# Spectral tiles as rows of one tile, with butterflies, mirror sums and filter products on two tiles an operation

## The chip, the cores and the metric

The kernel runs on one core of one Trainium2 chip. The metric is the device time of one execution in microseconds. The kernel before takes 454.19 us, the median of 3 runs (453.86 to 454.76). One further execution was taken with the hardware profiler; its own time was 452.46 us, and the span of its instructions 450.7 us. Line numbers such as L568 are lines of the kernel before, except in rows of the changed kernel's order, where they are lines of the changed kernel.

## The reference, cut to what matters

```python
xn = _layernorm(x, axis=-1)                     # x: [1, 2048, 448]
# branch A: a spectral filter
X = jnp.fft.rfft2(xn, axes=(-2, -1))
X = X * (w_r + 1j * w_i)                        # weights [2048, 225]
yA = jnp.fft.irfft2(X, s=(2048, 448), axes=(-2, -1))
# branch B: a gated network, F = 1792
gate = xn @ W_gate;  up = xn @ W_up
h = jnp.where(gate > 0, gate, 0) * up
yB = h @ W_down
return x + yA + yB
```

## The kernel before, in words

**Branch B is the long work of TensorE (PE).** Every fp32 product is made from fp16 parts (high times high, high times low, low times high). The 1792 hidden columns are cut into 14 blocks in groups of 5, 5 and 4, and the 2048 tokens into four chunks of 512. One *gate-and-up unit* is a block and a chunk: 20 to 24 matmuls of 512 columns into the two banks of a `gu` buffer, of which there are two. After it ScalarE (ACT) takes the relu (`g`, L1028), VectorE (DVE) multiplies by the up bank (`g`, L1032), ACT writes the high half of the result (`h`, L1036) and DVE the low half (`h`, L1040). The `gu` buffer is free again when the DVE's multiplication (L1032) has read it. The down products (`dn`, 448 columns) of a chunk follow when its group's units are through.

**Branch A is the background work.** Forward, each of 16 token residues has a transform along the columns and one along the sequence, on PE (`fx` banks); between them and behind them DVE does the rest in fp32: sums over eight rows (`eight_a`, `eight_b`, with the quarter turns in `turn`), and four levels of butterflies over the 16 residues (`f_y1`, `stage2`, `stage3`, `stage4`, all but the first through `bfly` and `rotate`). A spectral tile holds 464 fp32 numbers a partition: 8 column groups, 2 components (real, imaginary), 29 columns. There are 18 such buffers (`ybuf`), each a tile of its own, handed out from the list `free`. A DVE operation that treats the components apart works on 232 numbers, one on a whole tile on 464. Then each pair of frequencies k and k + 8 has its mirror sums (`pair`, through `add_sides`, with the other half fetched by DMA in `swap`), the product with the filter (`wmul`), and the way back: `inv1`, `stage2`, `stage3`. Row 32 of the partitions goes to a small side calculation (`row`), fetched by `row_in`.

**The last stage has eight steps p = 0 to 7.** Each takes the DVE chain of `i_join` (last butterfly, into a `wst` buffer), `i_pair`, `i_mix` in two halves (`eight_a`, `eight_b`), `i_lo` (`vt`, L815), then a sequence transform on PE (`i_sdft`, 48 matmuls of 64 columns, `fx<-im,vt`), ACT and DVE unfolding its result (`i_part`, L834; `i_unfold`, `yu`, L839), the halves of that (`i_pqhi` on ACT, L844; `i_pqlo` on DVE, `wf`, L849), and a column transform on PE (`i_ddft`, 48 matmuls of 56 columns, `fx<-idc_t,wf`). There is one pair of `fx` banks.

**What sets the order.** Opening and main loop give PE its units. The background stands in a list of items, each with a cost in microseconds (`bf` for butterflies, 1.09 to 1.74). At each unit a planner lets through as many items as its credit pays for. What is then recorded is reordered engine by engine by the framework's scheduler, and the result is a fixed queue for each engine: DVE cannot take a background item ahead of an L1032 that stands before it. All loads and stores are issued from SP's queue, in order.

## Time and profile before

| | |
|---|---|
| median of 3 runs | 454.19 us (453.86 to 454.76) |
| profiled execution, its own time | 452.46 us |
| its span | 450.7 us, mean granted TensorE clock 0.985 |
| PE busy | 427.8 us (95%), 3254 matmuls |
| DVE busy | 394.4 us (88%), 952 instructions |
| ACT busy | 252.8 us (56%), 508 instructions |
| POOL busy | 32.2 us (7%) |

The table is part 1 of the profile's page. Shares are averages over an opening (the first 15 us), a long middle in which PE and DVE are both busy, the eight steps of the last stage (from about 314 us), and an end in which PE works alone. The PE row says only that a matmul was under way; where PE is at its full rate a 512-column matmul starts every 0.216 us and a 448-column one every 0.189 us.

### The profile page before, as it was taken

To read this page: it belongs to the slowest core of one execution; us is meant where nothing else is said; L and a number is where in the kernel's file an instruction comes from. 1 tells how busy PE (TensorE), PEld (TensorE's weight loads), DVE (VectorE), ACT (ScalarE), POOL (GpSimd) and SP (SyncE) were. 2 spreads that over 40 slices of the span, in tenths; PEclk is the share of its full clock that TensorE was granted. 3 is DMA by queue.
4 is the path that set the end of the run, shared out by engine and by line. 5 is a ranking of instruction groups with operands and counts; after the bars stand their busy time and mean duration, and the time that the engine had idled before them with its cause. 6 is when DMAs were issued, how large, how long until landed. Compare 5 with 4: busy or idle time off the path is not lost.

```text
span 450.7 us, 8697 instructions
## 1 busy us (share of the span) xinstructions
PE 427.8 (95%) x3254; PEld 203.4 (45%) x3254; DVE 394.4 (88%) x952; ACT 252.8 (56%) x508; POOL 32.2 (7%) x72
## 2 busy tenths in 40 slices
PE   6999999999999999999999999979999973999997
PEld 2644544444444444444444444434545432444544
DVE  6898898997987998999999999999998989958513
ACT  6897392387359746615434553935675663563630
POOL 1140030031001401000000010010000000000000
PEclk9999999999999999999999999999999995999999
DMA  8769948015002235334330310022122112300212
GB/s 263 243 165 291 373 118 123 2 36 72 3 2 93 67 117 155 81 89 123 87 84 1 100 27 1 1 55 53 29 50 70 37 35 51 105 22 1 83 42 81
DMA packets 37722, 38.63 MB, mean 86 GB/s; under 512 B 18928, under 2 KB 33072, under 8 KB 37680
## 3 DMA queue, kind: packets, MB, share of 16 engines
q1 hardware_dynamic: 37680, 38.09, 30.8%
q8 instruction: 25, 0.41, 0.4%
q14 instruction: 17, 0.14, 0.1%
HBM read 23.20 MB, written 3.67 MB: 60 GB/s over the span
## 4 chain that ended last, share of the span: by engine, by line
PE 51%; DVE 38%; ACT 6%; issue 2%; DMA 2%; SPq 0%; DVEq 0%; ACTq 0%
PE gu L476 31%; PE dn L476 13%; PE fx L476 4%; DVE h L1040 3%; DVE g L1032 3%; DVE y L568 2%; DVE y L569 2%; DVE wt L928 2%; ACT junk L219 2%; DVE y L665 2%; DVE y L668 2%; DVE y L583 2%; DVE y L706 1%; DVE y L584 1%; DVE y L707 1%
## 5 line engine op out<-in xcount | busy, mean ns | idle before, releaser
L476 PE MATMUL gu<-T,wt 128*128 128x512 f16 (+2 forms) x1250 | 270.9, 377 | 4.5 <-DVE g L1032 4.5
L476 PEld LDWEIGHTS <-wt 128*128 128x128 f16 (+1 forms) x1250 | 111.4, 98 | 148.3 <-issue 29.1
L476 PE MATMUL dn<-wdt,h 128*128 128x448 f16 x624 | 127.5, 353 | 0.0
L476 PEld LDWEIGHTS <-h 128*128 128x128 f16 x624 | 60.2, 98 | 57.9 <-issue 0.8
L1036 ACT ACTIVATE h<-g 128x512 f16<-128x512 f32 x56 | 35.1, 627 | 76.7 <-DVE g L1032 76.6
L1032 DVE SCALAR_TENSOR_TENSOR g<-gu,g 128x512 f32<-128x512 f32 x56 | 38.2, 683 | 14.3 <-ACT g L1028 14.2
L1040 DVE TENSOR_TENSOR h<-g,h 128x512 f16<-128x512 f32 x56 | 38.3, 685 | 10.0 <-ACT h L1036 9.9
L1028 ACT ACTIVATE g<-gu 128x512 f32<-128x512 f32 x56 | 32.8, 585 | 17.7 <-PE gu L476 17.7
L1068 ACT ACTIVATE xy<-dn,dsc 128x448 f32<-128x448 f32 x44 | 27.3, 624 | 12.8 <-PE dn L476 12.8
L1057 ACT ACTIVATE dn<-xy,dinv 128x448 f32<-128x448 f32 x44 | 27.5, 631 | 0.5
L928 DVE SCALAR_TENSOR_TENSOR wt<-wst,wsc,wt 128x512 f16<-128x512 f32 x28 | 20.3, 742 | 2.6 <-ACT wt L924 2.6
L222 POOL PARTITION_ALL_REDUCE wm<-wm x15 | 9.0, 598 | 161.0 <-ACT junk L219 161.0
L924 ACT ACTIVATE wt<-wst,wsc 128x512 f16<-128x512 f32 x28 | 19.1, 713 | 1.8 <-DVE wsc L229 1.8
L219 ACT ACTIVATE junk<-wst 128x512 bf16<-128x512 f32 x28 | 17.4, 620 | 1.3 <-DMA wst<-in_wgu 1.1
L810 ACT ACTIVATE vt<-wst,fsc 128x928 f16<-128x928 f32 x8 | 8.8, 1099 | 10.8 <-DVE wst L467 10.8
L957 ACT ACTIVATE wdt<-wdst,wds 128x448 f16<-128x448 f32 x14 | 8.7, 658 | 8.5 <-DVE wds L953 8.5
L569 DVE TENSOR_TENSOR y<-y,y 128x464 f32<-128x464 f32 x21 | 13.3, 633 | 0.1
L568 DVE TENSOR_TENSOR y<-y,y 128x464 f32<-128x464 f32 x21 | 13.3, 632 | 0.1
L657 ACT ACTIVATE wf<-wf 128x116 f32<-128x116 f32 x16 | 4.5, 293 | 15.8 <-DMA wf<-in_wf 15.8
L839 DVE SCALAR_TENSOR_TENSOR yu<-fx,yu 128x512 f32<-128x512 f32 x16 | 11.0, 687 | 2.6 <-ACT yu L834 2.3
L860 ACT ACTIVATE fx<-xy,fsc 128x448 f32<-128x448 f32 x14 | 8.8, 629 | 7.9 <-DVE yu L839 7.9
L291 DVE BATCH_NORM_STATS2 bst<-y 128x6 f32<-128x448 f32 x16 | 9.2, 617 | 4.3 <-DMA y<-in_xr 4.3
(164 smaller groups left out, 506.2 us busy)
## 6 DMA issues: line engine op xcount, KB each, us to landing
wst<-in_wgu SPq DMA_DIRECT2D x28, 256.0 KB, 4.7
wf<-in_wf SPq DMA_DIRECT2D x16, 232.0 KB, 2.8
sw<-y SPq DMA_DIRECT2D x64, 58.0 KB, 2.0
sw<-wst SPq DMA_DIRECT2D x32, 116.0 KB, 2.2
y<-in_xr SPq DMA_DIRECT2D x16, 224.0 KB, 4.9
xy<-in_x SPq DMA_DIRECT2D x16, 224.0 KB, 5.0
out<-xy SPq DMA_DIRECT2D x15, 224.0 KB, 1.9
wdst<-in_wd SPq DMA_DIRECT2D x14, 224.0 KB, 4.6
```

The lines of the kernel that those rows point to most:

```text
L219: A.activation(mt([128, 512], BF16, "junk")[:, 0:src.shape[-1]], src, AF.Square, scale=SQ, accum_out=acc)
L476: r = P.matmul(*a, **k)
L568: V.tensor_tensor(t, a, b, op=OP.add)
L569: V.tensor_tensor(d, a, b, op=OP.subtract)
L924: A.activation(w[:, 0:4, :], wst[f, g], AF.Copy, scale=wsc[f, g])
L928: V.scalar_tensor_tensor(w[:, 4:8, :], st, sc, w[:, 0:4, :], op0=OP.mult, op1=OP.subtract)
L1028: last["A"] = A.activation(g1s[f, q], hps[f, q][:, 0, :], AF.Relu, scale=2.0 ** -22).ins
L1032: last["V"] = V.scalar_tensor_tensor(g1, hps[f, q][:, 1, :], 2.0 ** -22, g1, op0=OP.mult, op1=OP.mult).ins
L1036: A.activation(ht[f, q][:, 0, :], g1s[f, q], AF.Copy)
L1040: V.tensor_tensor(h[:, 1, :], g1s.pop((f, q)), h[:, 0, :], op=OP.subtract)
L1057: A.activation(dps[n2][:, 0:D], xy[n2], AF.Copy, scale=dinv[:, g:g + 1])
L1068: last["A"] = A.activation(xy[n2], dps[n2][:, 0:D], AF.Copy, scale=dsc[:, g:g + 1]).ins
```

## The change

The 18 spectral buffers become rows of one tile `yb`, and within a tile the components come first (2 components, 8 groups, 29 columns), so that one component is 232 numbers in a row. `joint` gives two buffers as one operand: any two rows of `yb`, in either order, are a regular stride. With that, `stage2`, `stage3`, `inv1`, `pair` and `wmul` take two tiles (928 numbers, or twice 232) in one DVE operation. A butterfly needs fewer buffers: its difference is written over one of its inputs. The tiles `eo` (two buffers) and `bw` become one tile `eb`, so that two of the three turns of the forward `eight_b` are done together. The joined butterflies come at other places of the list: `join2` for residues 0 and 2 at once (earlier 0 alone, then 2), for 1 and 3 at once, `join3` only then for the one half with all of its pairs; on the way back likewise. The planner's costs stay what they were for the same work (twice `bf` for a joined item). The low half `i_pqlo` is one operation of 1024 numbers. In `ln_lo` of two chunks a second DVE operation of 64 columns is replaced by a copy on ACT. `i_join`, whose output keeps the old layout, now needs four operations of 232 where it had two of 464, in six of its eight steps.

```diff
-    ybuf = [mt([128, NG, 2, KC], F32, f"y{i}") for i in range(18)]
+    yb = mt([128, 18, 2, NG, KC], F32, "y")
+    ybuf = [yb[:, i] for i in range(18)]
+    yi = {id(t): i for i, t in enumerate(ybuf)}
+    def joint(ts):
+        if len(ts) == 1:
+            return ts[0]
+        i, j = yi[id(ts[0])], yi[id(ts[1])]
+        return yb[:, i:j + 1:j - i] if j > i else (yb[:, i:j - 1:j - i] if j else yb[:, i::j - i])
...
-        for d, a, b in o:
-            if n2 % 4 in CHUNKS[2:]:
-                V.scalar_tensor_tensor(d, a, rst[n2 % 4, n2 // 4, "r"][0], b, op0=OP.mult, op1=OP.subtract)
-            else:
+        if n2 % 4 in CHUNKS[2:]:
+            d, a, b = o[0]
+            V.scalar_tensor_tensor(d, a, rst[n2 % 4, n2 // 4, "r"][0], b, op0=OP.mult, op1=OP.subtract)
+            A.activation(w[:, 8], w[:, 16], AF.Copy)
+        else:
+            for d, a, b in o:
                 V.tensor_tensor(d, a, b, op=OP.subtract)
...
+            u, v = (both[:, i:j + 1:j - i] for i, j in ((fi + 5, wi + 3), (fi + 6, wi + 7)))
+            turn(lambda c: rows[:, :, x[c]], u, v[:, :, ::-1], sgn)
...
-    def bfly(a, b, p, sgn):
+    def bflies(sa, sb, p, sgn):
+        st = [free.pop(0) for _ in sa]
+        a, b, t = joint(sa), joint(sb), joint(st)
         if p == 0:
-            t, d = free.pop(0), free.pop(0)
             V.tensor_tensor(t, a, b, op=OP.add)
-            V.tensor_tensor(d, a, b, op=OP.subtract)
-            free.extend((a, b))
-            return t, d
+            V.tensor_tensor(b, a, b, op=OP.subtract)
+            free.extend(sa)
+            return st, sb
...
+    def level(far, k, p, ks, sgn, src, dst, *js):
+        sa, sb = ([cur.pop((src, j + d, k)) for j in js] for d in (0, far))
+        for x, o in zip(ks, bflies(sa, sb, p, sgn)):
+            for j, t in zip(js, o):
+                cur[dst, j, x] = t
...
+        V.tensor_tensor(t, x, bc[0], op=OP.mult)
+        V.tensor_tensor(x, x, bc[1], op=OP.mult)
+        V.tensor_tensor(comp(t, 0), comp(t, 0), comp(x, 1), op=OP.subtract)
+        V.tensor_tensor(comp(t, 1), comp(t, 1), comp(x, 0), op=OP.add)
...
-    def pair(key, sgn):
-        add_sides(cur[key], sw.pop(key), sgn)
+    def pair(sgn, *keys):
+        add_sides(joint([cur[k] for k in keys]), sw.pop(keys[0]), sgn, comp)
...
-            V.scalar_tensor_tensor(o, t, f, a, op0=OP.mult, op1=OP.add)
-            V.scalar_tensor_tensor(d, t, -f, a, op0=OP.mult, op1=OP.add)
+            for c in range(2):
+                for x, g in ((o, f), (d, -f)):
+                    V.scalar_tensor_tensor(comp(x, c), comp(t, c), g, comp(a, c), op0=OP.mult, op1=OP.add)
...
-        y = yu.pop(p)
-        for b in range(2):
-            V.tensor_tensor(pgh[p + 8 * b][:, 1], y[:, b], pgh[p + 8 * b][:, 0], op=OP.subtract)
+        t = state["pg"]
+        V.tensor_tensor(t[:, 1], yu.pop(p), t[:, 0], op=OP.subtract)
...
-    extra = {1: [(ln_chunk, 1)], 2: [(join2, 0), (rows_in, 3)], 3: [(ln_chunk, 3)], 4: [(join2, 2), (join3, 2)],
-             6: [(join2, 1)]}
+    extra = {1: [(ln_chunk, 1)], 2: [(rows_in, 3)], 3: [(ln_chunk, 3)], 4: [(join2, 0, 2)]}
...
-    join2(3)
-    join3(3)
+    join2(1, 3)
+    join3()
```

The change also moves instructions, since the scheduler starts from other items. The built order of the two kernels differs at two places that matter for what follows. Both lie in the last stage, at the steps p = 3 and 4.

On DVE, before, from the unfolding of step 3 (`yu`) to the low half `i_pqlo` of step 3 (`wf`) and the L1032 of the next unit (`g_4918`):

```order
L1032 SCALAR_TENSOR_TENSOR g_4761<-gu,g_4761 128x512
L839 SCALAR_TENSOR_TENSOR yu<-fx,yu 128x512
L1040 TENSOR_TENSOR h<-g_4761,h 128x512
L839 SCALAR_TENSOR_TENSOR yu<-fx,yu 128x512
L444 TENSOR_TENSOR wst<-wst 128x2x232
L446 TENSOR_TENSOR wst<-wst 128x2x2x116
L448 TENSOR_TENSOR wst<-wst 128x3x116
L449 TENSOR_TENSOR wst<-wst 128x3x116
L849 TENSOR_TENSOR wf<-yu,wf 128x512 x2
L461 TENSOR_TENSOR wst<-wst 128x116
```

and in the changed kernel, the same stretch (L1064 is the multiplication that was L1032, L871 the unfolding, L881 the low half):

```order
L1064 SCALAR_TENSOR_TENSOR g_4611<-gu,g_4611 128x512
L1072 TENSOR_TENSOR h<-g_4611,h 128x512
L871 SCALAR_TENSOR_TENSOR yu<-fx,yu 128x512 x2
L463 TENSOR_TENSOR wst<-wst 128x2x232
L1064 SCALAR_TENSOR_TENSOR g_4768<-gu,g_4768 128x512
L465 TENSOR_TENSOR wst<-wst 128x2x2x116
L467 TENSOR_TENSOR wst<-wst 128x3x116
L468 TENSOR_TENSOR wst<-wst 128x3x116
L881 TENSOR_TENSOR wf<-yu,wf 128x1024
L477 TENSOR_TENSOR wst<-wst 128x116
```

The multiplication of the next unit (`g_4768`) now stands ahead of the low half of step 3; before, it (`g_4918`) stood six rows behind it, past the end of the piece shown.

On ACT, before, the same stretch (L834 is `i_part`, L844 `i_pqhi`, L1028 the relu of a unit, L876 what moves the column transform's result out):

```order
L834 ACTIVATE yu<-fx 128x512
L1036 ACTIVATE h<-g_4761 128x512
L860 ACTIVATE fx<-xy,fsc 128x448
L844 ACTIVATE wf<-yu 128x1024
L860 ACTIVATE fx<-xy,fsc 128x448
L1028 ACTIVATE g_4918<-gu 128x512
L876 ACTIVATE xy<-fx,fsc 128x2x224 x2
L1036 ACTIVATE h<-g_4918 128x512
L810 ACTIVATE vt<-wst,fsc 128x32x29
```

and in the changed kernel (L866 is `i_part`, L877 `i_pqhi`, L1060 the relu):

```order
L866 ACTIVATE yu<-fx 128x512
L1060 ACTIVATE g_4768<-gu 128x512
L892 ACTIVATE fx<-xy,fsc 128x448
L877 ACTIVATE wf<-yu 128x1024
L892 ACTIVATE fx<-xy,fsc 128x448
L1068 ACTIVATE h<-g_4768 128x512
L908 ACTIVATE xy<-fx,fsc 128x2x224 x2
L842 ACTIVATE vt<-wst,fsc 128x32x29
```

The relu of that unit has moved from behind the high half of step 3 to directly behind `i_part`. On PE's queue the same shift reads as counts: between the sequence transform of step 3 and its column transform there were 24 `gu` matmuls and are now 4; the other 20 stand earlier. From there on PE's queue holds the same in both kernels: column transform 3, sequence transform 4, column transform 4 with nothing between them, then 20 `gu` and 4 `dn` matmuls, then sequence transform 5.

More of the change, by code (lines that the diff above doesn't have):

```diff
@@ L588, in f_y1 @@
+        free.extend(st)
+        return sb, sa
     def f_y1(n2):
@@ L767, in i_join @@
         a, b = cur.pop(("i3", 0, p)), cur.pop(("i3", 1, p))
[L768 removed]
+        o, d = (u[:, :, :, KC * i:KC * (i + 1)].rearrange("p g c k -> p c g k") for i in range(2))
         if p == 0:
```

220 lines of the change are left out of this document (111 added, 109 removed).

## The prediction

> **What bounds the kernel now.** I read the shares of the page first, then PE's waits, then the stretches around those waits, then single rows. In the page's list of engines the columns are busy time, share and instructions; its slices follow.
>
> ```profile
> PE 427.8 (95%) x3254; PEld 203.4 (45%) x3254; DVE 394.4 (88%) x952; ACT 252.8 (56%) x508; POOL 32.2 (7%) x72
> ...
>
> ```
>
> PE is never far from busy, DVE nearly so. What matters is therefore when PE stands still, and for whom. PE's waits (us in total, times, longest):
>
> ```profile
> PE gu L476 <- DVE g L1032: 4.5, 3, 2.8
> PE fx L476 <- ACT fx L860: 4.4, 1, 4.4
> PE fx L476 <- ACT vt L810: 3.7, 1, 3.7
> PE fx L476 <- DVE vt L815: 1.6, 1, 1.6
> ```
>
> Two kinds. In the long middle DVE is late three times with freeing a `gu` buffer, 4.5 us. And in the last stage PE waits about 10 us for the chain of steps 3 to 5. Stretches (length, busy time of PE, PEld, DVE, ACT, POOL, granted clock, DMA):
>
> ```profile
> 270.00:285.00 15.00, 15.00 (x77) 6.97 (x76) 14.87 (x42) 7.53 (x16) 0.71 (x1) 1.00 0.01 2
> 285.00:300.00 15.00, 12.16 (x60) 5.42 (x59) 14.90 (x34) 10.18 (x23) 1.54 (x2) 1.00 0.15 33
> 360.00:375.00 15.00, 9.33 (x154) 4.92 (x154) 13.66 (x31) 7.91 (x12) 0.00 (x0) 0.84 0.14 34
> 375.00:390.00 15.00, 10.45 (x159) 5.92 (x154) 13.82 (x32) 6.71 (x10) 0.00 (x0) 0.71 0.39 100
> 390.00:405.00 15.00, 15.00 (x165) 7.48 (x164) 10.19 (x24) 10.15 (x16) 0.00 (x0) 1.00 0.09 32
> ```
>
> Between 270 and 300 us DVE has next to no idle time: it limits by its sum of work. Between 360 and 390 us it idles 2.5 us and PE 10.2, and the clock falls: there a chain that goes from PE to ACT and DVE and back limits. From 390 us PE is alone at full rate. PE, in time, through that place (start, us, operation, [idle before]):
>
> ```profile
> 361.63 0.87 PE L476 MATMUL fx<-im,vt 64*128 64x64 f16 x48
> 362.44 5.03 PE L476 MATMUL gu<-T,wt 128*128 128x512 f16 x24
> ...
> 372.52 0.29 PE L476 MATMUL fx<-im,vt 64*128 64x64 f16 x4 [3.68 <-ACT vt L810]
> 374.45 1.36 PE L476 MATMUL fx<-im,vt 64*128 64x64 f16 x44 [1.65 <-DVE vt L815]
> 380.18 0.28 PE L476 MATMUL fx<-idc_t,wf 64*128 64x56 f16 x4 [4.37 <-ACT fx L860]
> 380.64 1.25 PE L476 MATMUL fx<-idc_t,wf 64*128 64x56 f16 x44 [0.18 <-DVE wf L849]
> 381.82 5.44 PE L476 MATMUL gu<-T,wt 128*128 128x512 f16 x20
> 387.10 0.92 PE L476 MATMUL dn<-wdt,h 128*128 128x448 f16 x4
> 387.95 0.87 PE L476 MATMUL fx<-im,vt 64*128 64x64 f16 x48
> ```
>
> The sequence transform of step 3 ends at 362.50, that of step 4 at 375.81, that of step 5 starts at 387.95. Between the first two stand 24 `gu` matmuls, between the others 20 and 4 `dn`; the rest of the time PE waits.
>
> **What the change saves on DVE.** DVE starts, one after the other (start, duration):
>
> ```profile
> 251.30 0.40 DVE L671 TENSOR_TENSOR y<-y,y 128x232 f32<-128x232 f32 x1
> 251.61 0.39 DVE L670 TENSOR_TENSOR y<-y,y 128x232 f32<-128x232 f32 x1
> ...
> 252.24 0.45 DVE L706 SCALAR_TENSOR_TENSOR y<-sw,mask,y 128x232 f32<-128x232 f32 x1
> 252.61 0.45 DVE L707 SCALAR_TENSOR_TENSOR y<-sw,mask,y 128x232 f32<-128x232 f32 x1
> 252.98 0.63 DVE L568 TENSOR_TENSOR y<-y,y 128x464 f32<-128x464 f32 x1
> 253.53 0.63 DVE L569 TENSOR_TENSOR y<-y,y 128x464 f32<-128x464 f32 x1
> ```
>
> From start to start 232 numbers take 0.31 us, 464 take 0.55, and 232 with the mask 0.37. So 232 numbers more cost 0.24, and 0.07 is paid per operation: two operations of 464 (1.10) become one of 928 (estimate 0.55 + 2 x 0.24 = 1.03). With the mask, two of 232 (0.74) become one of 464, which the last stage has:
>
> ```profile
> 358.69 0.69 DVE L706 SCALAR_TENSOR_TENSOR wst<-sw,mask,wst 128x464 f32<-128x464 f32 x1
> 359.30 0.69 DVE L707 SCALAR_TENSOR_TENSOR wst<-sw,mask,wst 128x464 f32<-128x464 f32 x1
> ```
>
> 0.61, so 0.13 less. Counted in the built order: 116 plain operations disappear into others (20 of L568/L569, 24 of L575 to L578, 16 in rotations, 32 in the filter product, 16 turns, 8 of L849), 116 x 0.07 = 8.1; 16 with the mask, 2.1; eight of 64 columns go to ACT, 8 x 0.2 = 1.6 (duration 0.292 less the 0.08 by which neighbours overlap in the rows above); `i_join` gains 12, -0.8. Then dependence: an operation that reads what the one just before it wrote starts later.
>
> ```profile
> L815 DVE SCALAR_TENSOR_TENSOR vt<-wst,fsc,vt 128x464 f16<-128x464 f32 x16 | 10.5, 698 | 2.3 <-ACT vt L810 2.3
> ...
> L388 DVE SCALAR_TENSOR_TENSOR tt<-y,rs,tt 128x64 f16<-128x64 f32 x8 | 2.3, 292 | 0.0
> ```
>
> ```profile
> 364.98 0.63 DVE L444 TENSOR_TENSOR wst<-wst 128x464 f32<-128x464 f32 x1
> 365.53 0.63 DVE L446 TENSOR_TENSOR wst<-wst 128x464 f32<-128x464 f32 x1
> 366.20 0.52 DVE L448 TENSOR_TENSOR wst<-wst 128x348 f32<-128x348 f32 x1
> ```
>
> L446 needs nothing of L444 and comes after 0.55; L448 needs L446 and comes after 0.67. Joined pairs stand next to what they depend on more often (the order has 77 such neighbours before, 92 after): 15 x 0.12 = 1.8 lost. **DVE has about 8.1 + 2.1 + 1.6 - 0.8 - 1.8 = 9.2 us less work.** That is no gain by itself; PE's idle time is what it can buy.
>
> The Trainium skill (VectorE: DVE Perf Modes, section The DRAIN you can't avoid) says that the next operation cannot start until the pipe is empty; by that a merged pair of 232 would save 2 x 0.39 - 0.63 = 0.15, and DVE some 17 us in place of 8.1. The rows disagree: L569 starts 0.08 before L568 has ended.
>
> **The middle.** The three stalls:
>
> ```profile
> 154.80 2.53 PE L476 MATMUL gu<-T,wt 128*128 128x512 f16 x11 [1.09 <-DVE g L1032]
> ...
> 258.63 1.67 PE L476 MATMUL gu<-T,wt 128*128 128x512 f16 x7 [0.57 <-DVE g L1032]
> ...
> 296.22 3.95 PE L476 MATMUL gu<-T,wt 64*128 64x512 f16 x19 [2.83 <-DVE g L1032]
> ```
>
> Most of the 9.2 us is saved ahead of or within this stretch, so the first two go: -1.7. The third comes of a burst:
>
> ```profile
> 281.29 0.68 DVE L1032 SCALAR_TENSOR_TENSOR g<-gu,g 128x512 f32<-128x512 f32 x1
> ...
> 295.48 0.69 DVE L1032 SCALAR_TENSOR_TENSOR g<-gu,g 128x512 f32<-128x512 f32 x1
> ```
>
> DVE works for all of the 14.2 us between these two. Summed by the start-to-start times above, the rows between them come to 13.5 in the old order and 13.4 in the new, against 10.2 of PE between the ends of the two units in both. So the burst is still there, and DVE still falls back by some 3 us in it; it only enters it less late. I take 0.4 of the 2.83 to stay. Sum of the middle: **-4.1**; bounds -3.0 (half of the third stays) and -4.5.
>
> **The last stage.** Here the change costs. The shown order moves 20 `gu` matmuls from behind the sequence transform of step 3 to ahead of it. Ahead, PE had no hole to fill; behind, they filled the wait for `i_pqlo` of step 3. The chain of waits has such a group at full rate:
>
> ```profile
> 302.38 4.32 PE gu L476 x20
> ```
>
> So that transform ends 4.3 us later, and the chain that follows does not get shorter. Before, from its end at 362.50 to the end of column transform 4 at 381.89: 19.4. After, link by link: to the unfolding 0.67; the DVE rows from the unfolding to the end of `vt` of step 4, with the durations above, 11.2 (before 11.8, since one low half `h` of a unit falls away and the L849 pair becomes one row of 1.13); the transform 0.9; 0.67 again; unfolding to `wf` 4.5; then column transform 4 can begin only when the whole of `wf` is there, 1.3 where before 0.8 was left: 19.2. Then 20 `gu` and 4 `dn` as before. **Sum: 4.3 - 0.2 = +4.1**; bounds: +2.9 (the chain without the g and h of the moved unit, which may fall into a wait) and +5.7 (the clock, below).
>
> Where the edits cost nothing: the eight ACT copies lie in an engine that is 44% idle; loads and stores keep their sizes. A new wait: a butterfly's difference now overwrites an input that `row_in` may still be fetching. Behind residues 7 and 15 the joined difference stands one operation (1.03) after the fetch is issued.
>
> ```profile
> row<-y SPq DMA_DIRECT2D x16, 1.8 KB, 2.2
> ```
>
> With 2.2 to landing, DVE stands 1.2 us once, with the multiplications of the next units queued behind it, which by then have more room than that.
>
> **Sum.** -4.1 + 4.1 = 0 against the profiled 452.46 us (span 450.7). The median of the runs is 1.73 above that execution, so the forecast is the median, **454.2 us**.
>
> **Rivals.** *The middle's gain stays whole* (chance 0.32): the moved matmuls stand where PE would have waited, or the last stage enters with DVE so far ahead that its chain shortens. For it: PE had single waits ahead too; 9.2 us are much. Against: between 300 and 360 us the page's slices have PE at 9. Price: -4.1, so 450.1. *Slower through the clock* (0.24): with 4 matmuls in place of 24 PE idles three times for 4 to 5 us in a row in place of twice, the clock falls earlier and comes back later. In the rows above 20 `gu` took 5.44 at 381.82 and would take 4.32 at full clock; the granted clock came back 3.6 us after PE did. If it takes 6.8, 1.6 more is lost: 455.8. It decides from about 1 us on. The Trainium skill (TensorE: Matmul & The Clock Gate, Part 1) tells of a free-running window of about 3.4 us after which an idle array is halved and a busy one restored; by it the return takes 3.4 to 6.8, which is this rival; the 3.6 of the trace agrees with its lower end. *The joined operations don't do what they say* (0.06): rows of one tile lie far apart, and if two rows cost more than 0.48 together nothing is saved. Then the middle keeps its 4.5 and the last stage its +4.1: 458.3. No row of before shows such an operand of two far rows; operands in strides of 29 numbers (L815 above, 698 ns) take what the 0.69 of L706 in the last stage is, which speaks against it.
>
> **How the numbers follow.** No change 0.38, the three rivals 0.32, 0.24, 0.06. What a measurement can tell from no change is about 0.2%, 0.9 us. The forecast's own range, from the bounds, is -1.6 (+2.9 with -4.5) to +2.7 (+5.7 with -3.0): 452.6 to 456.9. To hold 8 in 10 it must reach to the first rival: 450.0 to 457.0. Faster 0.32, within 0.2% 0.38, slower 0.30.
>
> **What would show it.** Right: DVE busy near 385 us with some 824 instructions; rows of 2 x 464 near 1.1 us long; PE's wait for L1064 (L1032 before) under 1 us in all; the wait between sequence transforms 3 and 4 longer by about 4 us, and spread on three waits, one of them of column transform 3 for `wf`. Wrong: sequence transform 3 ending well before 362 us, or the wait of steps 3 to 5 no longer than the 10 us of before, or new waits of PE for DVE ahead of 300 us.

## The result, and the profile after

The changed kernel takes **458.71 us** (median of 4 runs, 458.67 to 459.0); the kernel before, run beside it, 454.48 (453.86 to 455.41). The ratio is 1.0093, with a 95% interval of 1.0074 to 1.0112: slower by 0.9%. The forecast was no change, 454.2, and the range ended at 457.0. The profiled execution took 459.0 us itself, its span is 457.2; that of before was 450.7, and the rows below account for these 6.5 us. The medians lie only 4.2 us apart: the profiled execution of the kernel before was a fast one, 2.0 us under the median beside it, at a mean granted clock of 0.985, where the more usual runs of that kernel show 0.981 and 453.7 us or more.

The page's list of engines says that DVE got what it was to get, 385.2 us in 824 instructions:

```profile
PE 431.3 (94%) x3254; PEld 204.2 (45%) x3254; DVE 385.2 (84%) x824; ACT 255.6 (56%) x516; POOL 30.4 (7%) x72
```

PE's waits in the changed kernel (us in total, times, longest; L1064 is the product that was L1032, L892 and L842 are ACT's steps that were L860 and L810):

```profile
PE fx L499 <- ACT fx L892: 4.4, 1, 4.4
PE fx L499 <- DVE wst L467: 3.9, 1, 3.9
PE fx L499 <- ACT vt L842: 2.9, 1, 2.9
PE gu L499 <- DVE g L1064: 2.7, 1, 2.7
PE fx L499 <- DVE wf L881: 2.0, 2, 1.3
...
PE fx L499 <- DVE vt L847: 1.1, 1, 1.1
PE dn L499 <- ACT dn L1089: 0.9, 1, 0.9
```

Two of the three stalls for DVE's product are gone, but the large one is there as it was, and in the last stage PE now waits 3.9 and 1.3 us around the start of column transform 3, where the kernel before waited 0.23. Stretches of the changed kernel (length, busy PE, PEld, DVE, ACT, POOL, granted clock, DMA):

```profile
285.00:300.00 15.00, 12.33 (x54) 5.11 (x52) 14.92 (x25) 9.72 (x21) 1.57 (x2) 0.89 0.15 33
...
360.00:375.00 15.00, 9.74 (x177) 5.35 (x175) 13.71 (x30) 8.50 (x14) 0.00 (x0) 0.86 0.16 37
375.00:390.00 15.00, 5.95 (x105) 3.66 (x104) 14.55 (x40) 7.15 (x10) 0.00 (x0) 0.50 0.21 54
390.00:405.00 15.00, 15.00 (x160) 7.55 (x159) 11.16 (x25) 7.34 (x11) 0.00 (x0) 0.96 0.23 64
```

The clock now falls in the middle too (0.89, where before had 1.00), and around 380 us it stands at one half for the whole stretch. PE in time through that place (start, us, operation, [idle before]):

```profile
366.99 0.88 PE L499 MATMUL fx<-im,vt 64*128 64x64 f16 x48
367.70 0.60 PE L499 MATMUL gu<-T,wt 64*128 64x512 f16 x4
372.24 0.28 PE L499 MATMUL fx<-idc_t,wf 64*128 64x56 f16 x4 [3.94 <-DVE wst L467]
373.83 1.21 PE L499 MATMUL fx<-idc_t,wf 64*128 64x56 f16 x44 [1.31 <-DVE wf L881]
377.95 0.29 PE L499 MATMUL fx<-im,vt 64*128 64x64 f16 x4 [2.91 <-ACT vt L842]
379.29 1.35 PE L499 MATMUL fx<-im,vt 64*128 64x64 f16 x44 [1.06 <-DVE vt L847]
385.02 0.28 PE L499 MATMUL fx<-idc_t,wf 64*128 64x56 f16 x4 [4.37 <-ACT fx L892]
386.01 1.21 PE L499 MATMUL fx<-idc_t,wf 64*128 64x56 f16 x44 [0.72 <-DVE wf L881]
387.15 6.46 PE L499 MATMUL gu<-T,wt 128*128 128x512 f16 x20
...
394.30 0.87 PE L499 MATMUL fx<-im,vt 64*128 64x64 f16 x48
```

These rows and those of before cut the 6.5 us in three:

- *Ahead of sequence transform 3* (the middle). It started at 361.63 and now starts at 366.99. Of the 5.36 us, 4.32 are the 20 `gu` matmuls that now stand ahead of it. The rest, **+1.0**, is lost.
- *From sequence transform 3 to sequence transform 5* (the last stage). Before 361.63 to 387.95, 26.3 us; now 366.99 to 394.30, 27.3, though it holds 20 matmuls fewer: 27.3 + 4.3 - 26.3 = **+5.3**.
- *Behind that*: 450.7 - 387.95 = 62.75 before, 457.2 - 394.30 = 62.9 now, **+0.15**.

In the middle, two rows show waits and lost time:

```profile
256.69 0.73 PE L499 MATMUL dn<-wdt,h 128*128 128x448 f16 x3 [0.94 <-ACT dn L1089]
...
295.58 6.66 PE L499 MATMUL gu<-T,wt 64*128 64x512 f16 x24 [2.67 <-DVE g L1064]
```

PE waits 2.67 us for the same product as before (2.83), and then the 24 matmuls run at a lower clock: 6.66 us, where the same 24 took 5.03 in the kernel before, behind the longer wait:

```profile
296.22 5.03 PE L476 MATMUL gu<-T,wt 64*128 64x512 f16 x24 [2.83 <-DVE g L1032]
```

So the clock is 1.6 us of the middle, and without it the middle would have gained 0.6. DVE's two products around that wait are as far apart as ever, 14.0 us (14.2 before):

```profile
280.82 0.68 DVE L1064 SCALAR_TENSOR_TENSOR g<-gu,g 128x512 f32<-128x512 f32 x1
...
294.84 0.69 DVE L1064 SCALAR_TENSOR_TENSOR g<-gu,g 128x512 f32<-128x512 f32 x1
```

Where DVE's saving went can be read from the stretches up to the first of these two products (columns as above; first the kernel before, then the changed one):

```profile
15.00:220.00 205.00, 203.91 (x1428) 94.09 (x1428) 188.42 (x472) 125.53 (x273) 24.59 (x54) 1.00 0.42 112
220.00:281.29 61.29, 60.72 (x301) 27.44 (x299) 60.85 (x146) 27.63 (x65) 3.04 (x4) 1.00 0.19 51
```

```profile
15.00:220.00 205.00, 205.00 (x1434) 94.64 (x1434) 178.13 (x393) 128.01 (x281) 21.39 (x54) 1.00 0.40 111
220.00:280.82 60.82, 59.85 (x296) 26.94 (x295) 59.42 (x97) 28.18 (x65) 4.39 (x4) 1.00 0.20 55
```

Up to 220 us DVE has 10.3 us less work, but PE had only 1.1 us of idle time there to win back. DVE is idle for longer instead, and at 220 us it has nearly as much left to do up to the product as before (59.4 and 60.9 us). The first product then starts 2.76 us ahead of PE's next run of 32 `gu` matmuls (280.82 and 283.58), where it was 2.75 before (281.29 and 284.04). DVE comes into this stretch just as late as it did.

### The profile page after: what moved, and what is told of

Its sections match the earlier page's. It is cut to its first block, busy times and chain, and to the rows that moved or that the text cites. A ratio compares the mean times of both kernels' runs of the same rounds, so it can differ in the third digit from the quotient of the medians.

```text
span 457.2 us, 8556 instructions
## 1 busy us (share of the span) xinstructions
PE 431.3 (94%) x3254; PEld 204.2 (45%) x3254; DVE 385.2 (84%) x824; ACT 255.6 (56%) x516; POOL 30.4 (7%) x72
## 4 chain that ended last, share of the span: by engine, by line
PE 65%; DVE 23%; DMA 4%; SPq 3%; ACT 2%; issue 1%; POOL 0%; DVEq 0%; ACTq 0%
PE gu L499 41%; PE dn L499 16%; PE fx L499 5%; DMA sw<-y 2%; SPq L725 2%; DVE y L593 2%; DVE g L1064 2%; DVE y L592 1%; DVE y L605 1%; DVE h L1072 1%; DMA wf<-in_wf 1%; DVE y L606 1%; DVE y L733 1%; PE dn L1128 1%; DVE y L691 1%
## 5 line engine op out<-in xcount | busy, mean ns | idle before, releaser
L1064 DVE SCALAR_TENSOR_TENSOR g<-gu,g 128x512 f32<-128x512 f32 x56 | 38.3, 683 | 18.7 <-ACT g L1060 18.5
L1060 ACT ACTIVATE g<-gu 128x512 f32<-128x512 f32 x56 | 32.9, 587 | 28.9 <-PE gu L499 28.6
L1100 ACT ACTIVATE xy<-dn,dsc 128x448 f32<-128x448 f32 x44 | 27.3, 624 | 15.0 <-PE dn L499 14.9
L1089 ACT ACTIVATE dn<-xy,dinv 128x448 f32<-128x448 f32 x44 | 27.4, 631 | 0.5
L960 DVE SCALAR_TENSOR_TENSOR wt<-wst,wsc,wt 128x512 f16<-128x512 f32 x28 | 20.6, 744 | 1.6 <-ACT wt L956 1.6
L499 PE MATMUL fx<-idc_t,wf 64*128 64x56 f16 x384 | 8.1, 194 | 10.3 <-ACT fx L892 4.4
L871 DVE SCALAR_TENSOR_TENSOR yu<-fx,yu 128x512 f32<-128x512 f32 x16 | 11.1, 691 | 6.3 <-ACT yu L866 6.1
L554 ACT ACTIVATE Xh<-eb 128x464 f16<-128x464 f32 x16 | 8.8, 586 | 13.3 <-DVE eb L490 13.2
L539 DVE SCALAR_TENSOR_TENSOR eb<-fx,y 128x464 f32<-128x464 f32 x16 | 9.5, 632 | 7.3 <-ACT y L527 7.3
L842 ACT ACTIVATE vt<-wst,fsc 128x928 f16<-128x928 f32 x8 | 8.8, 1100 | 8.6 <-DVE wst L490 8.6
L593 DVE TENSOR_TENSOR y<-y 128x928 f32<-128x928 f32 (+1 forms) x11 | 11.8, 1076 | 1.7 <-issue 1.6
```

The costliest lines, as they stand in the source:

```text
L499: r = P.matmul(*a, **k)
L593: V.tensor_tensor(b, a, b, op=OP.subtract)
L871: V.scalar_tensor_tensor(y[:, b], ps[:, 1], (-1.0) ** b * 2.0 ** -14, y[:, 1], op0=OP.mult, op1=OP.add)
L960: V.scalar_tensor_tensor(w[:, 4:8, :], st, sc, w[:, 0:4, :], op0=OP.mult, op1=OP.subtract)
L1060: last["A"] = A.activation(g1s[f, q], hps[f, q][:, 0, :], AF.Relu, scale=2.0 ** -22).ins
L1064: last["V"] = V.scalar_tensor_tensor(g1, hps[f, q][:, 1, :], 2.0 ** -22, g1, op0=OP.mult, op1=OP.mult).ins
```

## The theories

- **A**: the last stage's loss goes by how much other work of PE stands in the gaps between its transforms, and by nothing else. **B**, its rival: an operation on two tiles is itself dear at the end of a chain, since its consumer waits for both.
- **C**: the middle's gain was eaten by new waits of DVE (the reads of the row, 1.6 us; the swapped sides, 2.6). **D**: DVE has as much work per unit there as PE, so that a wait taken away comes back elsewhere. **E**, formed after the first runs: what matters is only what is queued on DVE between two products at one place.

All ratios below are to the kernel before, run on the same chip, with 95% intervals.

## Experiment: column transform 4 taken later, in both kernels

```diff
-        state["job"] = (state["at"], fn, a, 6.0)
+        state["job"] = (state["at"], fn, a, 10.0 if fn is i_ddft and a[0] == 4 else 6.0)
```

In the changed kernel:

> The changed kernel, with one number different: column transform 4 may be taken between two units only 10 us after it was offered, not 6, so that it no longer stands right behind sequence transform 4. Everything ahead of sequence transform 3 keeps its place on PE; behind it 12 to 40 gate/up and down matmuls now stand between any two transforms. Theory A (the place of the units did it): the five waits around column transform 3, sequence transform 4 and column transform 4 (14.3 us in the changed kernel's trace) and the half clock behind them (20.4 us of rows at half speed) go, less some 3 us for a new wait of the last column transform, which has only 11 gate/up matmuls ahead of it: 458.7 - 18 + 3, about 443 us (438 to 447), and within 2.5 us of the kernel before with the same number changed. Theory B (an operation on two tiles is itself dear at the end of a chain, since its consumer waits for both): the waits move but stay, and this one remains 4 us or more slower than the kernel before with the same number changed.

In the kernel before:

> The kernel before, with the same one number different (column transform 4 may be taken 10 us after its offer instead of 6). It too has sequence transform 4 and the two column transforms beside it in one run, with 24 gate/up matmuls in the gap ahead. Theory A: it loses 13.65 us of half clock and some 8 us of waits there, so it gains less than the changed kernel from the same edit: 454.5 - 12 + 3, about 445 us (441 to 449). Theory B: about the same 445 us, but the changed kernel stays 4 us or more above it.

Measured: the changed kernel so edited 448.0 us (0.9868, 0.9839 to 0.9897), 1 us above its range, the kernel before so edited **441.28** (0.9735, 0.9705 to 0.9765). The cluster of waits is gone in both; in the kernel before, PE no longer stands in that place and the clock stays whole:

```profile
360.00:375.00 15.00, 15.00 (x162) 7.19 (x161) 13.73 (x31) 8.70 (x14) 0.00 (x0) 1.00 0.13 30
375.00:390.00 15.00, 15.00 (x166) 7.59 (x164) 13.11 (x30) 9.88 (x16) 0.00 (x0) 1.00 0.27 72
```

But the two are 6.7 us apart, and by what was written down that speaks for B. The rows say otherwise. Sequence transform 3, with the moved matmuls taken off, starts at 367.60 - 4.32 = 363.3 in the one and at 361.3 in the other: 2 us are the middle's. And most of the rest is at the very end, where the edit brought the changed kernel another order. There the last pair of transforms has 11 short matmuls of the end between them, and the last 12 stand behind it:

```profile
432.87 0.87 PE L499 MATMUL fx<-im,vt 64*128 64x64 f16 x48
433.68 1.23 PE L1128 MATMUL gu<-wdt,h 128*128 128x224 f16 x11
438.11 0.23 PE L499 MATMUL fx<-idc_t,wf 64*128 64x56 f16 x4 [3.21 <-ACT fx L892]
...
440.92 2.40 PE L1128 MATMUL fx<-wdt,h 128*128 128x224 f16 x12 [1.31 <-ACT xy L908]
```

The kernel before has 43 matmuls in that last gap and waits only for the 1.31. The changed kernel's end has 3.7 us more of waits, and its last 12 matmuls take 2.40 us, where those of the kernel before take 1.31. The 3 us that I had allowed for the end were too few, since its waits come in a row. So the pair does not decide between A and B; the runs that follow do.

## Experiment: two-tile operations issued as two

```diff
-        i, j = yi[id(ts[0])], yi[id(ts[1])]
...
+        return list(ts)
...
+        for x in zip(*(t if isinstance(t, list) else [t] for t in (o, a, b))):
+            V.tensor_tensor(*x, op=op)
```

> The changed kernel with each butterfly, mirror sum and filter product on two tiles issued as two operations on one tile, one behind the other; layout, buffers and places stay. DVE's busy time rises from 385 to about 393 us. In the last stage the order then has 13 gate/up matmuls between sequence transform 3 and column transform 3 (4 in the changed kernel, 24 before). Theory A: the time goes by that number: halfway between the two kernels, 456.6 us (455 to 458.7), although DVE has 8 us more work. Theory B (two-tile operations are dear): 454.5 or less. A third way: DVE's 8 us come back onto the path and it is slower than the change, 460 or more.

Measured: 455.38 us (1.0037, 1.0016 to 1.0058). DVE is busy for 5.7 us more than in the changed kernel (390.9 and 385.2; 8 had been expected), and the time is 2.5 us *less* (by the two ratios). The edit leaves the low half `i_pqlo` (L881) and the joined turns in one operation, so it doesn't test B for these. The rows of its last stage:

```profile
364.11 0.87 PE L509 MATMUL fx<-im,vt 64*128 64x64 f16 x48
364.92 2.66 PE L509 MATMUL gu<-T,wt 128*128 128x512 f16 x13
...
390.68 0.87 PE L509 MATMUL fx<-im,vt 64*128 64x64 f16 x48
```

13 matmuls in the gap, and 26.6 us from sequence transform 3 to 5. That is the length of the two other kernels (26.3 with 24 in the gap, 27.3 with 4). The stretch has a length of its own, set by the chain, and each matmul that stands in its gap is free: what leaves it is paid in full. The time lies between the two kernels, as A has it, somewhat below the middle; B's bound of 454.5 was not reached, but not missed by much. The runs with the weights' splits, below, are sharper.

## Experiment: the last unit for spectral work two earlier

```diff
-LASTGU = 9
+LASTGU = 11
```

In the changed kernel, then in the kernel before, then in the changed kernel with 4 transfers a swap (the edit is shown in the next section):

> The changed kernel with the planner's last unit for spectral work two earlier (11 for 9). Now between any two transforms of the last stage stand at least 4.9 us of gate/up and down matmuls (in the changed kernel 0.9, 0 and 0 in three gaps running), and 22 down matmuls and more behind the last one. Theory A (what is lost there goes by the work that stands in the gaps, and nothing else): of the 19.6 us lost from 345 us on, some 3.5 stay: 458.7 - 16, about 442.6 us (440 to 446). Theory B (two-tile operations make each chain there longer, whatever stands in the gaps): waits of PE for ACT's and DVE's spectral pieces stay in most gaps, 447 or more.

> The kernel before with the same constant (11 for 9). Its gaps hold at least 4.8 us too, but the last column transform stands behind the down matmuls of the end. Theory A: about what the kernel before gave with column transform 4 taken later, 441.3 us (439 to 444), and the changed kernel with the same constant within 2.5 us of it, since both have filled gaps now. Theory B: the changed kernel stays 4 us or more above it.

> The changed kernel with that constant (11 for 9) and the sides of two tiles swapped by 4 transfers of both tiles instead of 8 of one. With theory C the waits for swapped sides fall from 2.6 to about 1.2 us, as in the run on waits, the wait for DVE's product near 295 us loses about 1 us, and the time is 0.5 to 1.5 below the run without the 4 transfers: about 441.6 us (439 to 445). Rival D: no difference between the two, within 0.7.

Measured: 450.68 us (0.9922, 0.9893 to 0.995), 442.83 (0.976, 0.9729 to 0.979) and 449.98 (0.9917, 0.9885 to 0.9948). The first is 8 us above what was expected and 7.9 above the kernel before with the same constant, which by what was written down speaks for B again; the third missed its range as well. In the last stage the expectation held, PE waits there for nothing of the spectral chain. But its largest waits are now of other lines:

```profile
PE fx L499 <- ACT fx L507: 6.1, 2, 4.8
PE fx L499 <- DVE eb L539: 4.9, 1, 4.9
```

L507 and L539 belong to the forward transforms, at 115 to 129 us: there the constant had put three of them side by side, with nothing between. I had looked at the gaps of the last stage alone. It is the same loss at another place, and the constant is too blunt a tool to say what the change is worth. The 4 transfers made no difference that can be told (the two runs' ranges overlap). That decides little between C and D, since PE waits for DVE's product only 0.4 and 0.3 us in these two runs, and there was little to take away.

## Experiments on the middle: waits taken away

With 4 transfers of both tiles for a swap, and the row's reads issued behind their forward transforms:

```diff
-        for n, key in enumerate(keys):
-            for o, i in PAIRS:
-                nc.sync.dma_start(t[o, n], cur[key][i])
+        x = joint([cur[k] for k in keys])
+        for o, i in PAIRS:
+            nc.sync.dma_start(t[o], x[i])
...
-            for j in (q, q + 4):
-                add(0.0, row_in, j)
...
+                add(0.0, row_in, seq[k - 1])
```

> The changed kernel, with the two new waits of DVE in the middle taken out: the reads of the row tile start right behind the forward transforms of their tiles (not just ahead of the butterflies that overwrite them), and the sides of two tiles are swapped by 4 transfers of both tiles instead of 8 of one. Theory C (the middle's gain was eaten by new waits): DVE's waits of 1.6 us at the butterfly and 2.6 us for the swapped sides fall below 0.8 together, the gate/up matmuls' one wait of 2.7 us for DVE's product ahead of 300 us shrinks to under 1, and the time falls by about 2.5 us to 456.2 (454.5 to 457.5). Rival D (DVE simply has as much work per unit there as PE, and the waits lie in time that it would have waited anyway): the waits go, the 2.7 us stay, 458.7 within 0.8. Theory A says that the last stage stays as it is in both cases, some 22 us lost there.

Without the row's reads at all:

```diff
-            nc.sync.dma_start(row[j + 8 * par:j + 8 * par + 1], cur["s1", j, par][ROW:ROW + 1])
+            if (j, par) == (0, 0):
+                G.memset(row, 1.0)
```

> The changed kernel without the reads of the row tile (so the row that it keeps apart comes out of a constant, and that row of the result is another); its order on PE is that of the changed kernel, matmul for matmul, so only DVE's wait of 1.6 us at the butterfly that overwrites a tile in place can differ. Theory C (new waits ate DVE's lead in the middle): the wait at the butterfly goes, the gate/up matmuls' wait of 2.7 us for DVE's product near 295 us falls by about 1.6 to 1.1, the dip of the granted clock behind it (0.97 in 235 to 300 us) becomes smaller or goes: 458.7 - 1.6 - 0 to 1.7, about 456.3 us (455.2 to 457.3). Rival D (the lost lead would have been waited away anyway): the 2.7 us stay and the time is 458.7 within 0.7. Under both the last stage keeps its 18.6 us of loss between the start of column transform 3 and the end of the matmuls behind column transform 4.

And, later, the 4 transfers alone:

> The changed kernel with only the 4 transfers of both tiles in place of 8 of one; the gap ahead of column transform 3 holds 4 gate/up matmuls as in the changed kernel. If the swaps hold the middle's lost gain, sequence transform 3 starts about 4 us earlier (363 us, counting none of the moved matmuls) and the time is near 454.5; if they hold only their own waits (2.6 us, of which DVE keeps about 1), it starts 1 to 2 us earlier and the time is 457.2 (456.3 to 458.0), as in the run on waits.

Measured: 457.24 us (1.0087, 1.0059 to 1.0115), 458.99 (1.0098, 1.0066 to 1.013) and 459.3 (1.0117, 1.0075 to 1.016).

The first run did only half of what it was made for. DVE's wait for the swapped sides fell to 1.2 us, but the wait at the butterfly is still there (1.8 us, 1.6 in the changed kernel), and the last two reads of the row are still issued at 169 us. Its order on PE is that of the run with the 4 transfers alone, and on DVE too but for one pair of neighbours. So it is in effect that run, and its time, inside the range for C, says nothing of the row; PE's wait for the product was to fall under 1 us and is 2.07. The third run missed its range (456.3 to 458.0) and its sign: sequence transform 3 starts at 367.15, not earlier than in the changed kernel (366.99). Both hold the same fall of the clock (below), so the 0.6 us that PE waits less for the product did not come through to the last stage.

Without the reads DVE's wait at the butterfly is gone and its order is the same, operation for operation, yet PE waits 2.66 us at 295.52, as in the changed kernel (2.67). DVE's 1.5 us of lead at 172 us had melted by 217 us. Its waits from 160 to 300 us are longer for the swapped sides (3.1, in the changed kernel 2.6) and new for the high halves of a down weight:

```profile
DVE y L733 <- DMA sw<-y: 3.1, 3, 1.7
DVE wdt L994 <- ACT wdt L990: 0.8, 2, 0.5
```

So C falls for the row: the lead was waited away by what came next. For the swaps C is right in kind and small in size. SP takes 0.59 us to issue a transfer of one tile and 0.60 for one of two, so 4 in place of 8 should bring the sides some 2.3 us earlier (an estimate from these; one row each of the changed kernel and of the run with 4 transfers alone; minimum, median and maximum in ns):

```profile
L725 SPq DMA_DIRECT2D sw<-y x64: 512/588/767, 192.5 to 256.5; - x64
```

```profile
L725 SPq DMA_DIRECT2D sw<-y x32: 546/597/667, 193.9 to 255.3; - x32
```

DVE's wait for them falls from 2.6 to 1.2 us, but PE's wait for the product only from 2.67 to 2.06.

The first and the third run also show something that no theory had: they have the same wait at the same place, and one of them pays 1.7 us more for it. First the row of the run with both edits, then that of the 4 transfers alone:

```profile
295.06 5.03 PE L499 MATMUL gu<-T,wt 64*128 64x512 f16 x24 [2.07 <-DVE g L1064]
```

```profile
295.04 6.72 PE L499 MATMUL gu<-T,wt 64*128 64x512 f16 x24 [2.06 <-DVE g L1064]
```

The clock fell behind the wait in the one execution and not in the other. The single runs without the row's reads lie in two groups, 456.94 and 457.26 with mean granted clocks of 0.976 and 0.978, and 458.99 to 459.26 with 0.973. So some 2 us of the changed kernel's time probably hang on whether the clock falls behind a wait of 2 to 2.8 us (the faster runs without the row's reads have no trace, so this rests on their mean clocks and on the two rows above); all four of its own runs lie near the upper group, and the medians of 457.2 and 459.3 above differ by no more than this.

## Experiments on the middle and the last stage: the splits of the last weights

DVE's queue between the two products around the wait held five splits of weights (L960, 0.75 us each). They were made due one unit later, one unit earlier, and one unit earlier together with the 4 transfers:

```diff
-            sched(gslot(s, 4) + g, w_hi, f, g)
-            sched(gslot(s, 4) + g, w_lo, f, g)
+            sched(gslot(s, 3) + g, w_hi, f, g)
+            sched(gslot(s, 3) + g, w_lo, f, g)
```

(5 in place of 3 for the earlier ones.)

> The changed kernel with the splits of the last weights (0.75 us each on DVE) due one gate/up unit later (3 units ahead of their use instead of 4). In DVE's queue between the products of gate/up units 36 and 37 stand 2 of them now, not 5. Theory E (the wait of 2.7 us near 295 us comes from what is queued there between two products, 13.4 us of DVE work over 10.6 us of PE, not from DVE's lead): 2.2 us less is queued, the wait falls under 0.7 us and the dip of the clock behind it goes, so that PE has lost some 15.5 us at the end of the middle (19.2 in the changed kernel). Rival D (DVE has as much work per unit there as PE, so the wait only moves to the next product): it has lost 18 or more there. In the last stage the gap ahead of column transform 3 now holds nothing (4 gate/up matmuls in the changed kernel): theory A gives that stage 1 us more. Sum under E and A: 458.7 - 3.7 + 1, about 456.0 (454.5 to 457.5); under D 459 to 460.

> The changed kernel with the same splits due one unit earlier (5 instead of 4 ahead) and the sides of two tiles swapped by 4 transfers instead of 8. What matters: its order in the last stage is that of the kernel before, 24 gate/up matmuls between sequence transform 3 and column transform 3, then nothing in the next two gaps. Theory A (the loss there goes by the work in the gaps): that stage loses the 13.2 us of the kernel before and not the 18.6 of the changed one, with all two-tile operations in place: 458.7 - 5.4 and 1 to 3 less in the middle: about 451 us (449 to 453.5), faster than the kernel before. Theory B (two-tile operations are dear at the end): the stage keeps 17 us or more, 455 or above.

> The changed kernel with only the splits of the last weights due one gate/up unit earlier; the gap ahead of column transform 3 holds 7 gate/up matmuls (4 in the changed kernel), which is 0.6 us of filler more. Theory E (the place of the splits holds the middle's lost gain): the wait of 2.7 us near 295 us and the clock's dip behind it go, as in the run with both edits: 458.7 - 0.6 - 3.5, about 454.6 (453.3 to 456.0). Otherwise another product waits in its place, 457.5 or more.

Measured: later 456.97 us (1.0054, 1.0029 to 1.0079), inside the range, though PE's wait, which was to fall under 0.7 us, is 1.18, and three splits stand between the products where two were expected; earlier with the transfers **451.03** (0.9935, 0.991 to 0.996), as expected; earlier alone **453.36** (0.9988, 0.997 to 1.0007), 1.2 below the figure expected, at the low end of its range, and no longer to be told from the kernel before.

The last two have every two-tile operation of the change in place. First the one with the transfers: 24 matmuls in the gap again, sequence transform 3 at 358.34, 3.3 us earlier than before in the same order:

```profile
358.34 0.87 PE L499 MATMUL fx<-im,vt 64*128 64x64 f16 x48
359.15 5.03 PE L499 MATMUL gu<-T,wt 128*128 128x512 f16 x24
...
386.27 0.87 PE L499 MATMUL fx<-im,vt 64*128 64x64 f16 x48
```

Then the earlier splits alone: 7 in the gap, so that 17 are ahead that were not, and 361.57 - 17 x 0.216 = 357.9, 3.7 us earlier:

```profile
361.57 0.87 PE L499 MATMUL fx<-im,vt 64*128 64x64 f16 x48
362.38 1.36 PE L499 MATMUL gu<-T,wt 128*128 128x512 f16 x7
...
388.90 0.87 PE L499 MATMUL fx<-im,vt 64*128 64x64 f16 x48
```

DVE's two products there are 10.4 us apart (14.0 in the changed kernel), and PE waits for neither:

```profile
279.52 0.69 DVE L1064 SCALAR_TENSOR_TENSOR g<-gu,g 128x512 f32<-128x512 f32 x1
...
289.89 0.69 DVE L1064 SCALAR_TENSOR_TENSOR g<-gu,g 128x512 f32<-128x512 f32 x1
```

All nine kernels with this cluster side by side. The second column counts the `gu` matmuls between sequence transform 3 and column transform 3; "less moved" is the start of sequence transform 3 less those that stand ahead of it and not behind, as against before (0.216 us each; for the gap of 0, 4.75 for all 24, of which 4 are half passes). The last two columns are the distance of DVE's two products around 290 us and PE's wait for the second.

| kernel | in the gap | seq. 3 starts | less moved | seq. 3 to seq. 5 | of that the 20 `gu` | products apart | PE waits |
|---|---|---|---|---|---|---|---|
| before | 24 | 361.63 | 361.6 | 26.3 | 5.44 | 14.2 | 2.83 |
| changed | 4 | 366.99 | 362.7 | 27.3 | 6.46 | 14.0 | 2.67 |
| no row reads | 4 | 366.99 | 362.7 | 27.6 | 6.71 | 14.0 | 2.66 |
| 4 transfers | 4 | 367.15 | 362.8 | 27.4 | 6.50 | 13.3 | 2.06 |
| 4 transfers, reads moved | 4 | 365.48 | 361.2 | 27.0 | 6.10 | 13.3 | 2.07 |
| operations split | 13 | 364.11 | 361.7 | 26.6 | 5.80 | 12.8 | 2.06 |
| splits later | 0 | 365.26 | 360.5 | 26.8 | 6.26 | 12.6 | 1.18 |
| splits earlier, 4 transfers | 24 | 358.34 | 358.3 | 27.9 | 6.44 | 11.5 | 0.24 |
| splits earlier | 7 | 361.57 | 357.9 | 27.3 | 6.59 | 10.4 | 0 |

Two things can be read off. The stretch from sequence transform 3 to 5 takes 26.3 to 27.9 us with 0 to 24 matmuls in its gap, and without its 20 `gu` at the end 20.5 to 21.5: that is the chain, whatever stands in its gap, and the rest of the difference is the clock behind it. This is A. B falls but for 0.6 us: with the same 24 in the gap, the chain takes 21.5 us with the joined operations (splits earlier, 4 transfers) and 20.9 in the kernel before. The second part of column transform 4 waits 0.72 us there for the joined low half (L881), where it waited 0.18 for the second of two operations.

And PE's wait follows the distance of the two products, falling from 2.83 to nothing between 14.2 and 10.4 us: this is E, as far as that wait goes. In the column "less moved", the changed kernel, the one without row reads and the one with 4 transfers hold the clock's fall of 1.6 to 1.7 us; without it they would stand near 361.1. What the edit of the splits did is not only to move splits: between those two products stood five before the edit, four with the earlier ones, and the rest of the distance is spectral work that the scheduler placed elsewhere. Which of the two, I did not take apart.

## Experiment: both faults out

The splits one unit earlier and column transform 4 taken later, in the changed kernel with the 4 transfers, and in the kernel before:

> The last one, and column transform 4 taken 10 us after its offer instead of 6, so that no two transforms of the last stage stand side by side; the last column transform has 14 down and 24 gate/up-bank matmuls ahead of it and the last 12 behind it. Theory A: the loss in the last stage falls from some 13 to 1, and about 1.5 come back at the very end: 451 - 12 + 1.5, about 440 us (437.5 to 442.5).

> The kernel before with column transform 4 taken 10 us after its offer and the splits of the last weights due one unit earlier. Theory A and E: 441.3 us (that with the later offer alone) less 0 to 3 for the wait near 295 us: about 440 us (438 to 442). Together with the run before this one it says what the change is worth when the gaps of the last stage are filled in both: between -2 and +2 us under theory A, 4 us dearer or more under theory B.

Measured: **438.82** us (438.67 to 439.17; 0.9662, 0.9631 to 0.9693) and 441.63 (440.73 to 442.66; 0.9724, 0.9688 to 0.9759). The first is the fastest kernel of all, 3.4% under the kernel before. With filled gaps and the splits earlier, the change is worth 2.8 us (with its 4 transfers): the opposite of B's 4 us dearer, and a little past the 2 us that had been written down as A's bound. The prediction had 4.1 for the middle. Of PE's waits beyond the opening, the changed kernel keeps these two of more than 0.3 us:

```profile
PE gu L499 <- DVE g L1064: 1.4, 3, 1.0
PE fx L1128 <- ACT xy L908: 1.3, 1, 1.3
```

and the kernel before, so edited, waits for DVE's product still:

```profile
PE gu L476 <- DVE g L1032: 2.6, 3, 1.4
```

In the kernel before, the earlier splits add nothing to the later column transform: 441.63 us with them, 441.28 without. The wait near 295 us did shrink there, from 2.84 to 0.55 us. But PE now waits 0.71 us at 188 us and 1.35 at 314, the 24 matmuls behind the latter take 6.70 us at a lower clock, and sequence transform 3 starts at 362.58 where it was 361.30. So in the kernel before the wait came back elsewhere, as D has it. E alone does not pay: in these runs the edit of the splits gained time only together with the work that the change takes off DVE. And part of the 2.8 us can be that fall of the clock, which the traced run of the changed kernel does not have.

## Why the prediction was wrong, step by step

- **DVE's saving, 9.2 us: right.** 394.4 to 385.2, in 824 instructions; rows of 928 numbers took 1.12 us at the median, where near 1.1 was foretold, and the next operation starts 1.04 us behind such a row (at 282.02 us, for one), where 1.03 was estimated.
- **The middle, -4.1: this is the step that failed.** It came out as +1.0. The first stall (1.09) went, as said. The second (0.57) went too, but 2 us earlier PE now waits 0.94 for ACT's seed of a down bank. The third I had seen as a burst of 13.5 us of DVE work over 10.2 of PE that "is still there", and then let DVE enter it so early that 0.4 of 2.83 stayed. It did not enter it early: 2.67 stayed, and its first product stands 2.76 us ahead of PE's next run, 2.75 before. The step took work saved on DVE for a lead that DVE keeps. The 10.3 us saved up to 220 us became idle time instead, at a place where PE had 1.1 us of idle time to win back. The run without the row's reads shows the same in small: 1.5 us of lead are waited away within 45 us. My own bound (half of the third stays) still assumed a lead. And a cost that I had only looked for in the last stage came on top, the clock behind that wait: 6.66 us for 24 matmuls that take 5.03. Without it the middle would be -0.6 in place of +1.0.
- **The middle's size, in principle: right.** With the queue at that place changed, sequence transform 3 starts 3.3 and 3.7 us earlier. Most of the 4.1 were there to be had, but not by the change alone.
- **The last stage, +4.1: right in its mechanism, a little small.** +5.3 came: 4.3 for the moved matmuls, and the chain as foretold (from the end of sequence transform 3, 367.87, to the end of column transform 4, 387.22: 19.35; predicted 19.2). The remaining 1.0 is the rival of the clock: the 20 `gu` behind it took 6.46 us, not 5.44.
- **The rival "slower through the clock"** had 1.6 us for this; 1.0 came there and about 1.6 in the middle. It was the case on the right side, but its time of 455.8 stood on the middle's -4.1 too.
- **The rival "the joined operations don't do what they say"** had 458.3 us, 0.4 from what was measured. That is luck: the joined rows took 1.12 us and DVE lost its 9.2 us of work, so the rival's reason did not come. It summed an unchanged middle and the last stage's +4.1, and the middle stayed for another reason.
- **The wait at the butterfly** was foretold as 1.2 us once, hidden; it was 1.6 and costs nothing, as the run without it shows.
- **What would show it**: PE's waits ahead of sequence transform 4 grew by 3.9 us (3.68 and 1.65 before; 3.94, 1.31, 2.91 and 1.06 after), as said, over four waits in place of three; the wait for L1064 under 1 us was the sign that failed.
- **The median on top of the profiled execution** (+1.7): the sum is 6.5 us off between the two profiled executions, but the forecast of the median only 4.5 off (458.71 and 454.2). The difference is that the profiled execution of before was faster than its median by 2.0 us, and that of the changed kernel slower by 0.3. The usual runs of the kernel before have the lower mean clock, so they may hold a fall of the clock in the middle too; none of them was traced, and this stays open.

## What to carry to other kernels

In these kernels, time saved on an engine that works through a fixed queue was worth something only where the next thing that another engine waits for moves forward in that queue, so look at what stands between two such things at the place of the wait, and not at the sum. Where a chain bounds a stretch, the other work inside it is free and what leaves it is paid in full: compare the built order around each chain before and after, since a rescheduled order can cost more than the edit saves. And once the change has been found slower, ask whether the two losses can be edited out apart from it; here that made the slower kernel the base of the fastest.

## What the runs showed of the hardware that was not expected

- A wait of PE of 2.06 us was followed by a lower clock in one execution (24 matmuls in 6.72 us) and not in another (5.03 us after 2.07), at the same place of nearly the same program; behind a wait of 2.83 in the kernel before, the clock stayed at 1.00, and in the kernel before with both edits it fell to 0.51 in the 2 us behind a wait of 1.35 (another wait, of 0.59, had ended 2.4 us ahead of that). The Trainium skill (TensorE: Matmul & The Clock Gate, Part 1) speaks of a free-running window of about 3.4 us and of one idle window before the clock is halved. That the outcome changes from execution to execution agrees with a window that runs free; that 2.06 us of idling were enough, and once less, does not agree with a whole idle window.
- The clock's return cost the 20 `gu` behind the chain between 1.1 and 2.4 us (5.44 to 6.71, where they take 4.32), with the same 20.5 to 21.5 us of chain ahead of them.
- A transfer costs SP's queue 0.59 us at the median to issue, whether it moves the rows of one tile or of two (0.60); by that, eight in a row are 4.7 us, and DVE waited for the swapped sides for up to 1.6 us in the changed kernel.
